# A packed-attention and expert-routing kernel: the first weight's partition layout, one slot's x turned by VectorE, and wide packing for three batches

## The chip, the cores and the metric

The kernel runs on one core of a Trainium2 chip. The metric is the device time of one execution in microseconds (us); where several runs are told, their median. Engines are named as in the profile: PE is TensorE's matmul, PEld its weight load, DVE VectorE, ACT ScalarE, POOL GpSimd, SP SyncE, which issues most of the transfers.

## The reference

Two attentions in a row, then a mixture of experts in which each token goes to one expert. B = 8 batches, 8 heads, 576 tokens, head size 64; 32 packing queries p; 8 experts, model width 512, hidden width 1024.

```python
def sm_attn(qq, kk, vv):                      # softmax(q k^T / 8) v
    ...
p_packed = sm_attn(p, k, v)                   # 32 packed rows per batch and head
out = sm_attn(q, p_packed, p_packed)
x = out.transpose(0, 2, 1, 3).reshape(B * S, H * D)        # 4608 x 512
logits = x @ w_gate + modality_bias[modality_id]
e_idx = argmax(logits); gate_w = softmax(logits)[e_idx]
for e in range(8):
    out[mask] = gate_w * (relu(x[mask] @ w1[e]) @ w2[e])   # mask: e_idx == e
```

## The kernel before, in words

**Attention.** The eight batches run as interleaved chains of small steps. The string ORDER writes out by hand in which order the steps of all batches stand on TensorE, VectorE, ScalarE and SyncE; it isn't changed. For each batch: transposes of k and q (L245), scores against p (L261), softmax, transposes of the probabilities (L285), `pack` (L307 or L301, with the scaling by VectorE at L314), `packT`, gate, scores of q against the packed rows (L261 again), a second softmax on VectorE, and `xpart` (L377), which makes x and the gate's logits. x goes to a scratch array in DRAM with one transfer per batch. `routing` (L447 and on) turns logits into list positions, and GpSimd scatters a record per token into lists by expert.

**The packing** has two forms. Narrow: four groups of matmuls with 64 input rows, 64 output rows and 128 columns, one for each pair of heads and half of the tokens. Wide: two groups with 64 input rows, 128 output rows and 256 columns, of which the two diagonal blocks are used. In the wide form VectorE's scaling takes the blocks one by one, four instructions on 64 partitions for two on 128. An fp32 matmul stands in the trace as two records. Before, `wide` held for batches 6 and 7.

**The slots.** Behind the attention, x is worked off in slots of tokens of one expert: slots 0 and 1 (256 tokens, from the first four batches, begun inside ORDER), slots 2 to 5 (256 tokens, from the first six), and then slots of up to 512 tokens. A slot fetches its rows of x by indirect DMA (L778) into `xt`, brings them into transposed order, splits them into a high and a low part (`hi` by ScalarE, `lo` by VectorE), runs `st_1` (three products with the split first weight w1) and `st_2` (three with w2), and scatters the result. Slots 0, 1 and 2 are turned by TensorE (`st_x`, L797): slots 0 and 1 through `first_x`, two tiles of 128 tokens each, and slot 2 through `st_x_both` between the two halves of slot 1's `st_2`. From slot 3 on VectorE turns them (`turn`, L813) in blocks of 32 by 32, 16 instructions for two tiles, one slot ahead, and `st_xs` (L819, L820) splits them.

**The first weight** is loaded by `load_w` with `which == 0`: 2 MB into `raw1`, from where ScalarE (L749) and VectorE (L753) split it. The order of its rows over partitions and blocks must fit that of x's columns. The scratch rows hold x as two halves u of 256 columns, so in `xt[:, t, u * HW:...]` heads lie in the order u, pair, block; the weight is fetched in that order, with eight transfers of 64 partitions.

Of the kernel before, what the change touches and what calls it, by code (L numbers as in the profile page):

```python
# [18 lines left out]
ds = bass.ds  # L19
# [5 lines left out]
def packed_attn_moe_kernel(  # L25
# [192 lines left out]
    def attention(b, lt, A, Z):  # L218
# [75 lines left out]
        def pack():  # L294
            a1T, v_t = D_["a1T"], D_["vr"]
            pp = [Z["ps1"].tile([P, 512], F32, name="ps1") for _ in range(2)]
            wide = b // 2 >= NA[1]
            for c in range(NC if wide else 0):
# [422 lines left out]
    def load_w(w, which, e):  # L721
        src, n = ((w1, KD), (w2, KF))[which]
        m = src.shape[2]
        if which == 0:
            d = w["raw1"].rearrange("p (h j f) -> p h j f", h=2, j=n)
            sv = src[ds(e, 1)].rearrange("e (a z u d) (h f) -> (e z) d h u a f", a=2, z=2, u=2, h=2)
            for h in range(2):
                for z in range(2):
                    for u in range(2):
                        ins = nc.sync.dma_start(d[64 * z:64 * z + 64, h, 2 * u:2 * u + 2], sv[z, :, h, u])  # L730
            return ins_of(ins)
        sv = src[ds(e, 1)].rearrange("a (j p) f -> p (a j) f", p=P)
        for z in range(2):
            ins = nc.sync.dma_start(w["2r"][z], sv[:, z * n // 2:(z + 1) * n // 2])
        return ins_of(ins)
# [24 lines left out]
    def fetch(tb, s, ph, mt, xt, n):  # L760
# [16 lines left out]
        def part(t, u):  # L777
            fetched.append(free(nc.gpsimd.indirect_dma_start(  # L778
                out=xt[:, t - 2 if t > 1 else 3 - t, u * HW:u * HW + HW], out_offset=None,
                in_=x_scr[0:NA[ph] * 4 * S] if ph < 2 else x_scr,  # L780
                in_offset=bass.IndirectOffsetOnAxis(ap=mt[:, t, 3 * u:3 * u + 1], axis=0))))
            return fetched[-1:]
# [12 lines left out]
    def st_x(xt, M, t, ps):  # L795
        for j in range(KD):
            nc.tensor.transpose(out=ps[:, j], in_=xt[:, t, j * P:j * P + P], identity=ident)  # L797
        yield
        ts = slice(t * P, t * P + P)
        hi, lo = (M["x"][z][:, :, ts] for z in range(2))  # L800
        ia = nc.scalar.copy(out=hi, in_=ps)
        yield
        iv = tt(out=lo, in0=ps, in1=hi.bitcast(F32), op=ALU.subtract)
        if slow[0]:
            feed(ia)
        M["ia"], M["iv"] = ins_of(ia), ins_of(iv)
        yield

    def turn(n, ts):
        g, x = (z[:, ts].rearrange("p t (j n) -> p (t j) n", n=P) for z in (xt_of(n), W["xt"][n >= SA[1]]))  # L810
        for z in range(0, P, Q):
            for w in range(0, P, Q):
                nc.vector.transpose(out=x[w:w + Q, :, z:z + Q], in_=g[z:z + Q, :, w:w + Q])  # L813

    def st_xs(M, ts):
        x = W["xt"][M is V].rearrange("p t (j n) -> p j t n", n=P)
        hi, lo = (M["x"][z].rearrange("p j (t n) -> p j t n", n=P) for z in range(2))
# [64 lines left out]

    def st_x_both(xt, M):
        for t in range(2):
            all_of(st_x(xt, M, t, W["t", t]))
        return M["ia"], M["iv"]

    def st_2(M, mt, t, op, parts=1):
# [29 lines left out]
    W["ot"] = [mxp.tile([P, DM], F32, name="ot")] * 2  # L918
    xts = [mxp.tile([P, 2, DM], F32, name=f"xt{n}") for n in range(2)]
    W["xt"] = [xts[0]]  # L920
    x_hl = mxp.tile([P, 2, KD, P2], F32R, name="x_hl")
# [5 lines left out]
    def slot_of(n):  # L927
        ph = sum(n >= z for z in first[1:])
        return T[ph]["tab"], n - first[ph], ph

    def xt_of(n):
        return xts[n % 2 if n < 3 else 1 if n < SA[1] else 2]
# [112 lines left out]
    for z, nm in enumerate(("kT", "qT")):  # L1045
# [3 lines left out]
                    "p (j n) -> p j n", j=KD)])  # L1049
    xts.append(wraw.tile([P, 4, DM], F32, name="xt2"))  # L1050
    W["xt"].append(spare("rawv", F32).rearrange("p (t f) -> p t f", t=4))
    W["ot"] = [W["ot"][0], wraw.tile([P, DM], F32, name="ot2")]

# [55 lines left out]
    def slot(n):  # L1109
# [4 lines left out]
        def x_next(done=()):  # L1114
# [3 lines left out]
            with ExitStack() as es:  # L1118
                for z in done:
                    es.enter_context(tc.issue_after(ins_of(z)))  # L1120
                after = st_xs(X, range(2 if n + 1 < SA[1] else 3))
                flag = n + 1 >= SA[1] and val(tn, sn, 6, (ET.Activation, ET.DVE), 0, 1)
            if n + 1 >= SA[1]:
                with tc.If(flag > 0):
                    turn(n + 1, slice(3, 4))
                    st_xs(V, (3,))
            return after

        if n < SA[1]:
            done = st_1_full(W)  # L1130
            if n == SA[0] - 1:
                st_2_of(n, (1, 0))
                sw(n + 1, 0, st_x_both(xts[0], X))
            else:
                sw(n + 1, 0, x_next(done))
                if n + 1 == SA[1]:
                    pending.extend(held)
                    flush()
            st_2_of(n, *(((0, 1),) if n == SA[0] - 1 else ((1, 0), (0, 1))))
        else:  # L1140
# [31 lines left out]
    def go_on(n):  # L1172
# [3 lines left out]
        if n < SA[1]:  # L1176
            if n >= SA[0]:
                turn_of(n + 1)
            pre(n + 2)
# [53 lines left out]
```

## Time and profile before

| | |
|---|---|
| time before, median of 3 runs | 565.15 us (564.54 to 567.61) |
| profiled execution | 566.15 us, span 564.5 us |
| busy share of the span: PE, DVE, ACT, POOL | 96%, 60%, 37%, 37% |
| granted TensorE clock, mean | 0.984 of 2.4 GHz |
| HBM read, written | 57.04 MB, 19.28 MB |

The span is that from the first to the last instruction; the profiled time holds 1.65 us more. Busy shares are means over stages with different limits: up to about 138 us the attention, behind it the slots.

### The profile page before, as it was taken

What the parts mean: (1) busy time and instruction counts of PE and PEld (TensorE: products, weight loads), DVE (VectorE), ACT (ScalarE), POOL (GpSimd) and SP (SyncE); (2) the same over time, 40 slices, a digit from 0 to 9 for tenths busy, and PEclk for the clock granted to TensorE, in tenths of its full rate; (3) what the DMA queues carried; (4) which work ended last, traced back from release to release, by engine and by line L of the source; (5) the groups of instructions that cost most, each with busy time, mean ns of one, the idle gap of its engine ahead of it and who ended that gap; (6) DMA issues with size and microseconds to landing.
All of it is one profiled execution on the core that took longest, in us unless ns stands there. A gap on an engine that the chain in (4) does not pass through costs nothing. (4 is left out here: it accounts for less than half of the span.)

```text
span 564.5 us, 11470 instructions
## 1 busy us (share of the span) xinstructions
PE 541.6 (96%) x4336; PEld 457.7 (81%) x4336; DVE 338.6 (60%) x760; ACT 208.9 (37%) x371; POOL 210.2 (37%) x257
## 2 busy tenths in 40 slices
PE   5999998978999999999999999999999999999995
PEld 4777777655989899899898888998888888988884
DVE  1399998997987275635576728339358148167210
ACT  2588886674532122221213224422212242422221
POOL 4002004843554445451542332473412422472402
PEclk9799999987999999999999999999999999999999
DMA  9699998993338611119621115424201210511501
GB/s 291 252 326 363 403 337 282 278 258 124 123 106 192 220 43 64 48 51 194 225 75 40 59 56 128 126 104 134 78 19 44 70 39 37 57 38 59 56 10 72
DMA packets 33684, 77.38 MB, mean 137 GB/s; under 512 B 6768, under 2 KB 6944, under 8 KB 32576
## 3 DMA queue, kind: packets, MB, share of 16 engines
q1 hardware_dynamic: 24224, 54.92, 30.5%
q0 software_dynamic: 8848, 21.28, 13.6%
q8 instruction: 43, 0.70, 0.5%
q14 instruction: 41, 0.34, 0.2%
q10 hardware_dynamic: 528, 0.13, 0.1%
HBM read 57.04 MB, written 19.28 MB: 135 GB/s over the span
## 5 line engine op out<-in xcount | busy, mean ns | idle before, releaser
L778 POOL DMA_INDIRECT xt<-x_scr,mt x86 | 85.4, 992 | 86.3 <-issue 24.5
L813 DVE STREAM_TRANSPOSE rawv<-xt 32x384 f32<-32x384 f32 (+1 forms) x192 | 92.3, 481 | 16.1 <-DMA xt<-x_scr,mt 12.3
L909 POOL DMA_INDIRECT out_dram<-ot,mt x37 | 37.3, 1008 | 138.8 <-ACT ot L898 94.3
L892 PE MATMUL ps_o<-rawq,rawk 128*128 128x512 f32 x272 | 87.2, 391 | 0.0
L856 PE MATMUL ps_h<-x_wide,w1h 128*128 128x512 f32 (+1 forms) x168 | 62.4, 371 | 0.0
L856 PE MATMUL ps_h<-x_wide,w1l 128*128 128x512 f32 (+1 forms) x168 | 61.9, 368 | 0.0
L856 PE MATMUL ps_h<-pT,w1h 128*128 128x512 f32 (+1 forms) x168 | 61.3, 365 | 0.0
L892 PEld LDWEIGHTS ps_o<-rawq,rawk 128*128 128x128 f32 x272 | 51.0, 188 | 10.4
L837 PE MATMUL ps_h<-x_hl,w1h 128*128 128x256 f32 x320 | 58.1, 283 | 0.1
L498 POOL DMA_INDIRECT lst<-meta,dsi x36 | 36.5, 1014 | 45.8 <-ACT lt L384 32.9
L837 PEld LDWEIGHTS ps_h<-x_hl,w1h 128*128 128x128 f32 x320 | 49.9, 189 | 0.6 <-DVEq L1079 0.3
L861 DVE SCALAR_TENSOR_TENSOR rawk<-ps_h,rawk 128x512 fp32r<-128x512 f32 (+1 forms) x28 | 17.4, 633 | 54.2 <-ACT rawk L860 54.0
L837 PE MATMUL ps_h<-x_hl,w1l 128*128 128x256 f32 x160 | 45.3, 284 | 0.0
L898 ACT ACTIVATE ot<-ps_o,mt 128x512 f32<-128x512 f32 x24 | 16.5, 688 | 67.8 <-PE ps_o L892 45.2
L892 PE MATMUL ps_o<-qT,rawk 128*128 128x512 f32 x96 | 37.5, 391 | 0.0
L856 PEld LDWEIGHTS ps_h<-pT,w1h 128*128 128x128 f32 x168 | 31.6, 188 | 4.1
L856 PEld LDWEIGHTS ps_h<-x_wide,w1l 128*128 128x128 f32 x168 | 31.4, 187 | 4.2
L856 PEld LDWEIGHTS ps_h<-x_wide,w1h 128*128 128x128 f32 x168 | 31.6, 188 | 3.9
L860 ACT ACTIVATE rawk<-ps_h 128x512 fp32r<-128x512 f32 (+1 forms) x28 | 15.2, 551 | 47.6 <-PE ps_h L856 46.6
L837 PEld LDWEIGHTS ps_h<-x_hl,w1l 128*128 128x128 f32 x160 | 30.2, 189 | 0.0
L892 PE MATMUL ps_t<-rawq,rawk 128*128 128x512 f32 x88 | 28.9, 389 | 0.0
L841 ACT ACTIVATE rawk<-ps_h 128x512 fp32r<-128x512 f32 x20 | 12.0, 599 | 43.4 <-PE ps_h L837 43.4
(268 smaller groups left out, 1134.2 us busy)
## 6 DMA issues: line engine op xcount, KB each, us to landing
rawq<-in_q_dram SPq DMA_DIRECT2D x8, 1152.0 KB, 9.4
rawv<-in_v_dram SPq DMA_DIRECT2D x8, 1152.0 KB, 9.6
x_scr<-xs SPq DMA_DIRECT2D x8, 1152.0 KB, 5.2
raw<-in_moe_w_dram SPq DMA_DIRECT2D x32, 256.0 KB, 7.0
rawk<-in_k_dram SPq DMA_DIRECT2D x7, 1152.0 KB, 11.7
kT<-in_moe_w_dram SPq DMA_DIRECT2D x4, 1024.0 KB, 5.5
qT<-in_moe_w_dram SPq DMA_DIRECT2D x3, 1024.0 KB, 8.1
xt<-x_scr,mt POOLq DMA_INDIRECT x86, 2.9
```

What stands on the lines that cost most here:

```text
L498: ins = ins_of(nc.gpsimd.indirect_dma_start(out=lst, out_offset=bass.IndirectOffsetOnAxis(ap=dsi[:, c:c + 1], axis=0), in_=meta[:, i * NC ...
L778: fetched.append(free(nc.gpsimd.indirect_dma_start(out=xt[:, t - 2 if t > 1 else 3 - t, u * HW:u * HW + HW], out_offset=None, in_=x_scr[0: ...
L813: nc.vector.transpose(out=x[w:w + Q, :, z:z + Q], in_=g[z:z + Q, :, w:w + Q])
L837: nc.tensor.matmul(ps[:, f], M[a][:, j, (f0 + f) * P:(f0 + f) * P + P], M["x"][b][:, j, 0:P2], start=(n == 0), stop=(n == 3 * KD - 1))
L841: ia = nc.scalar.activation(out=hid(M, "hh", f0), in_=ps, func=AF.Relu)
L856: nc.tensor.matmul(ps, M[a][:, j, f * P:f * P + P], M["x"][b][:, j, cs], start=(n == 0), stop=(n == 3 * KD - 1))
L860: ia = nc.scalar.activation(out=hh, in_=ps, func=AF.Relu)
L861: iv = nc.vector.scalar_tensor_tensor(out=hl, in0=ps, scalar=0.0, in1=hh.bitcast(F32), op0=ALU.max, op1=ALU.subtract)
L892: nc.tensor.matmul(op, hid(M, a, j, 1, slice(t * P, t * P + P))[:, 0], M[b][j // 4][:, j % 4], start=(n == 0), stop=(n == 3 * KF - 1))
L898: ia = nc.scalar.activation(out=ot, in_=op, func=AF.Copy, scale=mt.bitcast(F32)[:, row_of(t), 2:3])
L909: nc.gpsimd.indirect_dma_start(out=out, out_offset=bass.IndirectOffsetOnAxis(ap=mt[:, row_of(t), 1:2], axis=0), in_=M["ot"][t == 0], in_of ...
```

## The change

Four edits that hang together, in one diff:

- `load_w` fetches the first weight as two transfers of 128 partitions, in the natural order of its rows (row = block times 128 plus partition).
- So that x fits, `xt` is laid out as half u, tile t, column; a block of 128 columns of transposed x is made of 64 columns of each half. `st_x` makes each block with two matmuls against the identity, one for each half of the output partitions, instead of one transpose; `turn` reads the halves one by one, with as many instructions as before.
- Slot 2's x is turned by VectorE: `st_x_both` is gone, `turn` stands in slot 1's `x_next` behind slot 1's `st_1`, and both halves of slot 1's `st_2` follow each other. It turns into the first half of the buffer that the wide slots fetch into. Slot 3's `turn` is told to stand behind slot 2's last subtraction.
- `wide` holds for batches 5, 6 and 7.

```diff
-            wide = b // 2 >= NA[1]
+            wide = b >= 2 * NA[1] - 1
...
-            sv = src[ds(e, 1)].rearrange("e (a z u d) (h f) -> (e z) d h u a f", a=2, z=2, u=2, h=2)
+            sv = src[ds(e, 1)].rearrange("e (j p) (h f) -> p h (e j) f", p=P, h=2)
             for h in range(2):
-                for z in range(2):
-                    for u in range(2):
-                        ins = nc.sync.dma_start(d[64 * z:64 * z + 64, h, 2 * u:2 * u + 2], sv[z, :, h, u])
+                ins = nc.sync.dma_start(d[:, h], sv[:, h])
...
-                out=xt[:, t - 2 if t > 1 else 3 - t, u * HW:u * HW + HW], out_offset=None,
+                out=xt[:, u, t - 2 if t > 1 else 3 - t], out_offset=None,
...
         for j in range(KD):
-            nc.tensor.transpose(out=ps[:, j], in_=xt[:, t, j * P:j * P + P], identity=ident)
+            for u in range(2):
+                nc.tensor.matmul(ps[64 * u:64 * u + 64, j], xt[:, u, t, j * D:j * D + D], ident, start=True, stop=True)
...
-        g, x = (z[:, ts].rearrange("p t (j n) -> p (t j) n", n=P) for z in (xt_of(n), W["xt"][n >= SA[1]]))
-        for z in range(0, P, Q):
-            for w in range(0, P, Q):
-                nc.vector.transpose(out=x[w:w + Q, :, z:z + Q], in_=g[z:z + Q, :, w:w + Q])
+        x = turned(n)[:, ts].rearrange("p t (j n) -> p (t j) n", n=P)
+        for u in range(2):
+            g = xt_of(n)[:, u, ts].rearrange("p t (j d) -> p (t j) d", d=D)
+            for z in range(0, P, Q):
+                for w in range(0, D, Q):
+                    nc.vector.transpose(out=x[u * D + w:u * D + w + Q, :, z:z + Q], in_=g[z:z + Q, :, w:w + Q])
...
+    def turned(n):
+        return W["xt"][2 if n == SA[0] else n >= SA[1]]
...
+    W["xt"].append(xts[2].rearrange("p a b n -> p (a b n)").rearrange("p (t f) -> p t f", f=DM)[:, 0:2])
...
-                after = st_xs(X, range(2 if n + 1 < SA[1] else 3))
+                if n + 1 == SA[0]:
+                    turn(n + 1, slice(0, 2))
+                after = st_xs(X, n + 1, range(2 if n + 1 < SA[1] else 3))
...
+            W["iv"] = after[1]
             return after
...
             done = st_1_full(W)
-            if n == SA[0] - 1:
-                st_2_of(n, (1, 0))
-                sw(n + 1, 0, st_x_both(xts[0], X))
-            else:
-                sw(n + 1, 0, x_next(done))
...
-            st_2_of(n, *(((0, 1),) if n == SA[0] - 1 else ((1, 0), (0, 1))))
+            sw(n + 1, 0, x_next(done))
...
+            st_2_of(n, (1, 0), (0, 1))
...
             if n >= SA[0]:
-                turn_of(n + 1)
+                with tc.issue_after(W["iv"]) if n == SA[0] else ExitStack():
+                    turn_of(n + 1)
```

## Rows read from the trace of the kernel before

**Rows 1.** Busy time by stretch: engines' busy us, granted clock, DMA share, GB/s.

```profile
96.00:112.40 16.40, 15.33 (x235) 12.46 (x242) 15.01 (x37) 11.05 (x20) 13.96 (x32) 1.00 1.00 248
138.00:560.00 422.00, 419.82 (x2366) 365.54 (x2344) 234.20 (x520) 116.35 (x193) 166.87 (x166) 1.00 0.31 85
```

**Rows 2.** The same view of five short stretches (PE, PEld, DVE, ACT, POOL; PEclk, DMA, GB/s).

```profile
100.00:104.00 4.00, 3.83 (x71) 3.20 (x70) 3.79 (x7) 3.24 (x6) 3.63 (x9) 1.00 1.04 396
106.00:112.00 6.00, 6.00 (x102) 5.13 (x102) 5.60 (x13) 2.75 (x6) 5.04 (x7) 1.00 1.07 213
116.00:119.50 3.50, 3.50 (x36) 2.54 (x21) 3.43 (x6) 1.14 (x5) 2.89 (x3) 0.52 1.01 202
122.80:126.30 3.50, 1.72 (x25) 1.27 (x16) 3.33 (x6) 3.50 (x8) 0.00 (x0) 1.00 1.03 320
126.30:133.10 6.80, 6.57 (x30) 4.72 (x30) 4.87 (x14) 4.52 (x7) 2.08 (x3) 0.51 0.48 190
```

**Rows 3.** The first weight's transfers, 100 to 112 us: issue times, time to landing.

```profile
L730 SPq DMA_DIRECT2D raw<-in_moe_w_dram x8: 603/604/1114, 101.5 to 108.2; - x8
...
DMA to landing us min/median/max: 8.5/9.7/10.8
```

**Rows 4.** ScalarE's split of that weight: duration ns, first and last start.

```profile
L749 ACT CAST w1h<-raw x4: 1039/1052/1122, 121.5 to 129.0; 128x1024 fp32r<-128x1024 f32 x4
```

**Rows 5.** PE's instructions in order, 85 to 140 us: start, us, line, shapes.

```profile
90.69 0.48 PE L447 MATMUL ps<-lt,fold 128*64 128x72 f32 x8
91.10 1.09 PE L245 MATMUL ps<-ident,rawq 128*128 128x128 f32 x8
92.12 1.08 PE L307 MATMUL ps<-rawv,a1T 64*64 64x128 f32 x27
93.60 1.53 PE L307 MATMUL ps<-rawv,a1T 64*64 64x128 f32 x45 [0.40 <-issue]
...
106.69 4.16 PE L301 MATMUL ps<-rawv,a1T 64*128 64x256 f32 x36
...
127.20 7.78 PE L301 MATMUL ps<-rawv,a1T 64*128 64x256 f32 x36
```

**Rows 6.** DVE's instructions in order, 90 to 145 us.

```profile
95.17 0.35 DVE L314 SCALAR_TENSOR_TENSOR bd<-ps,r,mask 128x128 f32<-128x128 f32 x1 [1.14 <-PE ps L307]
...
112.47 1.44 DVE L314 SCALAR_TENSOR_TENSOR bd<-ps,r,mask 64x128 f32<-64x128 f32 x4 [0.70 <-PE ps L377]
...
128.31 0.17 DVE L451 TENSOR_TENSOR lg<-ps,bias_all 128x72 f32<-128x72 f32 x1
```

**Rows 7.** PE's instructions in order, 125 to 207 us, around the transposes of x.

```profile
139.65 1.09 PE L797 MATMUL ps<-ident,xt 128*128 128x128 f32 x8
140.68 1.62 PE L377 MATMUL ps<-bd,a2T 64*64 64x136 f32 x48
...
157.04 0.66 PE L797 MATMUL ps<-ident,xt 128*128 128x128 f32 x4
157.46 0.47 PE L892 MATMUL ps<-rawq,rawk 128*128 128x512 f32 x1
...
193.86 0.77 PE L837 MATMUL ps_h<-x_hl,w1h 128*128 128x256 f32 x5
```

**Rows 8.** DVE and ACT in order, 150 to 265 us: slots 1 and 2.

```profile
182.84 0.69 DVE L843 SCALAR_TENSOR_TENSOR rawk<-ps_h,rawk 128x512 fp32r<-128x512 f32 x1 [0.54 <-ACT rawk L841]
...
186.50 0.17 DVE L579 CAST tab_c<-tab_f 128x7 int32<-128x7 f32 x1
...
199.08 7.19 DVE L813 STREAM_TRANSPOSE xt<-xt 32x256 f32<-32x256 f32 x16 [0.45 <-DMA lst<-meta,dsi]
...
206.35 1.14 ACT L819 CAST x_hl<-xt 128x512 fp32r<-128x512 f32 x2 [0.17 <-DVE xt L813]
...
208.10 1.28 DVE L820 TENSOR_TENSOR x_hl<-xt,x_hl 128x512 fp32r<-128x512 f32 x2
```

More of the change, by code (lines that the diff above doesn't have):

```diff
@@ L809, in turn, with st_xs @@
     def turn(n, ts):
-        g, x = (z[:, ts].rearrange("p t (j n) -> p (t j) n", n=P) for z in (xt_of(n), W["xt"][n >= SA[1]]))
-        for z in range(0, P, Q):
-            for w in range(0, P, Q):
-                nc.vector.transpose(out=x[w:w + Q, :, z:z + Q], in_=g[z:z + Q, :, w:w + Q])
-    def st_xs(M, ts):
-        x = W["xt"][M is V].rearrange("p t (j n) -> p j t n", n=P)
+        x = turned(n)[:, ts].rearrange("p t (j n) -> p (t j) n", n=P)
[4 more added lines that the diff above has]
+                    nc.vector.transpose(out=x[u * D + w:u * D + w + Q, :, z:z + Q], in_=g[z:z + Q, :, w:w + Q])
+    def st_xs(M, n, ts):
+        x = turned(n).rearrange("p t (j n) -> p j t n", n=P)
         hi, lo = (M["x"][z].rearrange("p j (t n) -> p j t n", n=P) for z in range(2))
@@ L881, in st_1_full @@
         return M["last"]
[L883 to L886, printed above, removed]
     def st_2(M, mt, t, op, parts=1):
@@ L918, in packed_attn_moe_kernel @@
     W["ot"] = [mxp.tile([P, DM], F32, name="ot")] * 2
-    xts = [mxp.tile([P, 2, DM], F32, name=f"xt{n}") for n in range(2)]
-    W["xt"] = [xts[0]]
+    xts = [mxp.tile([P, 2, 2, HW], F32, name=f"xt{n}") for n in range(2)]
+    W["xt"] = [xts[0].rearrange("p a b n -> p (a b n)").rearrange("p (t f) -> p t f", f=DM)]
     x_hl = mxp.tile([P, 2, KD, P2], F32R, name="x_hl")
@@ L1049, in packed_attn_moe_kernel @@
                     "p (j n) -> p j n", j=KD)])
-    xts.append(wraw.tile([P, 4, DM], F32, name="xt2"))
+    xts.append(wraw.tile([P, 2, 4, HW], F32, name="xt2"))
     W["xt"].append(spare("rawv", F32).rearrange("p (t f) -> p t f", t=4))
+    W["xt"].append(xts[2].rearrange("p a b n -> p (a b n)").rearrange("p (t f) -> p t f", f=DM)[:, 0:2])
     W["ot"] = [W["ot"][0], wraw.tile([P, DM], F32, name="ot2")]
@@ L1125, in x_next @@
                     turn(n + 1, slice(3, 4))
-                    st_xs(V, (3,))
+                    st_xs(V, n + 1, (3,))
+            W["iv"] = after[1]
             return after
@@ L1130, in slot @@
             done = st_1_full(W)
-            if n == SA[0] - 1:
-                st_2_of(n, (1, 0))
-                sw(n + 1, 0, st_x_both(xts[0], X))
-            else:
-                sw(n + 1, 0, x_next(done))
-                if n + 1 == SA[1]:
-                    pending.extend(held)
-                    flush()
-            st_2_of(n, *(((0, 1),) if n == SA[0] - 1 else ((1, 0), (0, 1))))
+            sw(n + 1, 0, x_next(done))
+            if n + 1 == SA[1]:
+                pending.extend(held)
+                flush()
+            st_2_of(n, (1, 0), (0, 1))
         else:
```

## The prediction, made before the changed kernel ran

> **What bounds the kernel now.** The first view is the busy time of each engine by stretch. Behind 138 us TensorE works 419.8 of 422 us [rows 1]: the expert slots run as one unbroken stream of matmuls, so there the end moves only with the amount of TensorE work, or with a new wait put into the stream. Ahead of it, in the attention part, TensorE and VectorE are both nearly full (15.3 and 15.0 of 16.4 us from 96 to 112.4) [rows 1], and the order on each engine is written out by hand, so a delay there is passed on from batch to batch. The time is therefore: when the stream starts (about 138 us), what is added to it or taken from it, and the tail.
>
> The second view is the clock and the DMA traffic of short stretches [rows 2]. The reader is to see two things. The first weight moves at 213 GB/s while the DMA engines are fully busy, and other loads get 396 GB/s from equally busy engines. And TensorE's granted clock is 0.5 (1.2 GHz) in two stretches, 116 to 119.5 and 126.3 to 133.1, while it is 1.0 (2.4 GHz) in the others. Ahead of the second fall TensorE had worked 1.72 of 3.5 us. That second stretch covers the packing of the last batch, which took 7.78 us where the same 36 records of batch six took 4.16 [rows 5].
>
> The sum is made against the profiled execution: 566.15 us, a span of 564.5 and 1.65 around it. It lies 1.0 above the median of the three runs, 565.15. A difference of 0.5%, 2.8 us, is about what a measurement of this kernel can tell from no change: the bounds are 562.3 and 568.0.
>
> **The weight's load: 0.** Eight transfers of 256 KB on 64 partitions each become two of 1 MB on 128. 2.1 MB at 213 GB/s is 9.8 us, at 396 GB/s 5.3, so the weight lands some 4.5 us sooner, and SyncE issues six transfers fewer per weight at 0.6 us each [rows 2, 3]. Nobody waits for it: the last transfer is issued at 108.2 and the slowest took 10.8 us to land, so all is there by 119.0 [rows 3], and ScalarE's first split of it starts at 121.5, in its hand-written place [rows 4]. The three later loads lie under the full stream [rows 1]. If this cover were thinner than it looks, the gain would be at most those 4.5 us; I take 0. The list writes and x rows that share the DMA engines come sooner too, and this is what lets the stream start earlier, should TensorE get there earlier.
>
> **Batch five packed wide: +2.0.** The narrow packing of batch five runs from 92.12 to 95.13 with a pause of 0.40 in it; the wide one took 4.16 for batch six [rows 5]. That is +1.15, or +1.55 if the pause stays. VectorE stood waiting for it (1.14 us idle before 95.17) [rows 6], so its end is on the path. Behind it VectorE does four scalings for two; four took 1.44 us in batch six [rows 6], so two more are +0.7. Together 1.85 to 2.25. Queued behind them are the softmax steps of batches four to six and the next PSUM buffers, and with VectorE and TensorE both above 90% busy up to 112.4 there is little slack to swallow it. Bounds: 0 if all is swallowed, 2.3. I take 2.0, because the wait at 95.17 is seen.
>
> **Slot one's and two's x by matmuls: +1.5.** Eight transposes took 1.03 us (139.65 to 140.68) and four took 0.42 (157.04 to 157.46) [rows 7], so a tile costs 0.45 to 0.5. In its place come eight fp32 matmuls with 64 output rows, two records each. No such row exists with 128 columns. The nearest has the same 128x64 shape with 72 columns: eight records from 90.69 to 91.10, 51 ns each [rows 5]. Sixteen make 0.82, so +0.35 a tile and +1.4 for four; I take 1.5 for the longer rows of output. Below: the first two tiles hide behind VectorE, +0.7. Above: if the halves don't run side by side. Narrow packing has four side by side, 45 records in 1.53 us, 34 ns each [rows 5]; one at a time that is 136 ns, 2.2 us a tile, +6.8 in all.
>
> The Trainium skill speaks against this part: "TensorEngine Tiling (Array Packing)", section Tiling Modes, says that a change of tiling mode drains the TensorE. The trace doesn't show a drain: the 128x64 group of eight ends at 91.17, after the full-size transposes have started at 91.10, and so do the transposes at 140.74 against the 64x64 group at 140.68 [rows 5, 7]. As an estimate by that rule, each of eight changes would wait for the tail of the last matmul.
>
> **The third slot's x moves to VectorE: +0.5.** (Slot 2 in the code.) Eight transposes leave the stream: by the rows above 0.42 to 0.5 per four, so -0.9 [rows 7]. Slot 2's first matmul would come at 193.86 - 0.9 = 193.0 instead of 193.86 [rows 7]. Against it stand 16 block transposes on VectorE, 7.19 us as for the next slot [rows 8], then ScalarE's copies and VectorE's subtractions. They may start once slot 1's last hidden rows are done, at 183.53, or behind the table's last step, at 186.67 [rows 8]: they end at 190.7 to 193.9. One copy of 0.57 and both subtractions of 1.28 follow [rows 8], so x is ready at 192.6 to 195.8 and TensorE waits 0 to 2.8. The middle, 1.4, makes +0.5; bounds -0.9 and +1.9. What is queued behind: slot 3's block transposes, which now start at about 196 where they started at 199.08 [rows 8], so they are not late. The later slots do the same block transposes with the same sizes: 0.
>
> **The clock over the last packing: -2.6.** All of the last attention part shifts by 2 us, and whether TensorE falls to 1.2 GHz there turns on where its idle stretches fall; the rows can't settle it. At 2.4 GHz the last packing could still not run before VectorE has read the routing values that hold its second PSUM buffer, at 128.48 [rows 6]. From there it would need 3.9 (34 of 36 records of 4.16) and end at 132.4, not at 134.98 [rows 5]: -2.6. In the trace TensorE fell after a stretch half idle [rows 2]; with the wider packing it has a fuller schedule, and the earlier low stretch is not sure to come back either. So I take full clock as somewhat likelier than not.
>
> Sum: 566.15 + 2.0 + 1.5 + 0.5 - 2.6 = 567.55, so **567.5**, which is 0.4% above the median shown: no change that can be told.
>
> **The rivals.**
> *The clock falls again* (the case on the other side, slower). Place: TensorE while it packs the last batch. Price: the 2.6 are not got back, 570.2. It decides by itself: with full clock the sum is under 568.0, without it above. For it: the idle stretch before it has a cause that the change leaves alone, ScalarE being full (3.50 of 3.50 us) [rows 2]. Against: the shift.
> *The delay of batch five is swallowed*: -2.0, 565.5. For it: TensorE has a wait of its own after the narrow packing. Against: VectorE's 15.0 of 16.4 us.
> *All terms at their low ends* (faster): packing 0, first tiles +0.7, third slot -0.9, last packing -2.6, and the first low stretch gone as well, which gives back 3.5 x 0.48 = 1.7 if all of it was on the path [rows 2]. 566.15 - 4.5 = 561.6. Against: four things must go well.
> *The turn comes late on VectorE*: the full wait of 2.8, 568.9; if x comes later still, each us is one more.
> *A drained array at every change of shape*: a group's last record takes about 0.48 - 7 x 0.051 = 0.12 us [rows 5], two changes for each of four tiles, +1.0, 568.5. This is the mechanism of the rule on tiling modes named above; the overlapping starts in the trace speak against it.
> That the faster weight brings nothing is no rival here; it is in the sum.
>
> **How the numbers follow.** Forecast 0.38, the clock falls 0.22, delay swallowed 0.13, all low 0.13, late turn 0.09, drained array 0.05. Faster than 562.3: nearly all of "all low" and a little of the swallowed case, 0.14. Slower than 568.0: the clock case (0.21), most of the late turn and the drain (0.12) and the upper part of the forecast's own spread, 566 to 569 (0.11): 0.44. The rest, 0.42, is no change. The range reaches down into the all-low case and up past the clock case: 562.5 to 570.8. The upper bound of the matmul term (+6.8) lies outside it; I count it in the 2 of 10.
>
> **What would show it.** Right: the first weight's two transfers land within 6 us at about 390 GB/s; batch five's packing stands under the wide line with some 4.1 us and VectorE's scalings end about 2 us later; the first x tiles take some 0.8 us each; slot 2's first matmul waits for the subtraction, 1 to 2 us; the last packing takes 4 us behind its start and the clock there is 1.0. Wrong: if the stream starts more than 1 us before 138 in the new profile, the attention part had slack or a cost that I don't see; if TensorE's idle time behind 138 grows by over 3 us, the turn or the longer order on VectorE is the new bound; if a tile of x costs over 1.5 us, the halves don't run side by side.

## The result and the profile after

The changed kernel takes 573.04 us (median of 4 runs, 571.92 to 573.35) against 566.38 for the kernel before, run beside it (median of 4). The ratio is 1.0118, 95% interval 1.0091 to 1.0145: slower by 1.2%. The forecast was 567.5 with a range up to 570.8, so the time lies outside it on the slow side. The profiled execution took 573.19 us, its span is 571.2.

Lines move by the edit: the matmuls of x are L796, the first layer L838, the second L888, VectorE's block transposes L814. The first view is TensorE's timeline of the changed kernel (start, duration, line and operation, and in brackets the idle time before it and what ended it). It answers to [rows 5] and [rows 7].

```profile
93.25 4.16 PE L301 MATMUL ps<-rawv,a1T 64*128 64x256 f32 x36
...
99.37 0.41 PE L245 MATMUL ps<-ident,rawk 128*128 128x128 f32 x2 [0.90 <-PE ps L475]
...
127.46 1.97 PE L245 MATMUL ps<-ident,rawq 128*128 128x128 f32 x8 [2.07 <-ACT lt L384]
...
131.57 5.47 PE L301 MATMUL ps<-rawv,a1T 64*128 64x256 f32 x34 [0.30 <-DVE lg L451]
...
141.71 1.97 PE L796 MATMUL ps<-ident,xt 128*64 128x128 f32 x32
...
159.68 1.09 PE L796 MATMUL ps<-ident,xt 128*64 128x128 f32 x16
...
167.65 0.48 PE L447 MATMUL ps<-lt,fold 128*64 128x72 f32 x8
...
185.25 0.40 PE L888 MATMUL ps_o<-rawq,rawk 128*128 128x512 f32 x1
...
198.34 0.74 PE L838 MATMUL ps_h<-x_hl,w1h 128*128 128x256 f32 x4 [2.04 <-ACTq L1079]
...
199.67 0.58 PE L838 MATMUL ps_h<-x_hl,w1h 128*128 128x256 f32 x1 [0.60 <-DVEq L1079]
...
211.97 0.39 PE L888 MATMUL ps_o<-rawq,rawk 128*128 128x512 f32 x1
```

The same two marks of the second layer (slot 1's first matmul, slot 2's first) in the kernel before, and ahead of them the first transposes behind batch five's packing and the matmul that follows slot 1's x (L447):

```profile
96.08 0.44 PE L245 MATMUL ps<-ident,rawk 128*128 128x128 f32 x2 [0.27 <-DVE bd L314]
...
163.61 0.48 PE L447 MATMUL ps<-lt,fold 128*64 128x72 f32 x8
...
182.01 0.40 PE L892 MATMUL ps_o<-rawq,rawk 128*128 128x512 f32 x1
...
205.38 0.40 PE L892 MATMUL ps_o<-rawq,rawk 128*128 128x512 f32 x1
```

Four marks cut the span into stretches: the start of batch five's packing, slot 1's second layer, slot 2's second layer, the end. Before: 92.12, 182.01, 205.38, 564.5. After: 93.25, 185.25, 211.97, 571.2. The stretches grow by 1.13, 2.11, 3.35 and 0.11 us, together 6.7. Half of the loss stands between slot 1's and slot 2's second layers, the place where slot 2's x comes in. The first 1.13 lies ahead of every edited instruction.

The busy time of the engines in six stretches of the changed kernel (us; then busy time of each engine, the granted clock, DMA share and GB/s):

```profile
10.00:24.00 14.00, 10.45 (x76) 7.77 (x77) 4.23 (x9) 3.51 (x10) 1.73 (x3) 0.63 1.01 351
...
116.00:119.50 3.50, 1.76 (x44) 0.94 (x36) 3.39 (x8) 2.65 (x8) 2.59 (x4) 1.00 0.45 169
...
127.50:134.20 6.70, 6.39 (x30) 4.77 (x32) 6.35 (x16) 5.75 (x9) 3.96 (x4) 0.50 0.68 253
...
180.00:187.00 7.00, 7.00 (x54) 6.72 (x53) 5.22 (x24) 1.54 (x3) 4.62 (x5) 1.00 1.05 397
...
198.00:203.00 5.00, 4.07 (x21) 3.86 (x22) 4.76 (x14) 0.93 (x2) 4.07 (x4) 0.66 0.33 80
203.00:560.00 357.00, 357.00 (x1807) 310.69 (x1807) 188.17 (x355) 94.95 (x153) 134.96 (x135) 1.00 0.25 73
```

The low stretch from 116 to 119.5 is gone, and not only moved: from 112 to 126 the granted clock is 1.00 throughout. The clock still falls to 1.2 GHz over the last packing (0.50), as in [rows 2], and now once more behind the wait ahead of slot 2 (0.66 on average from 198 to 203). From 203 on TensorE is full.

Why does TensorE wait at 196 to 200? VectorE's timeline of the changed kernel, around the turn of slot 2's x:

```profile
186.08 0.69 DVE L844 SCALAR_TENSOR_TENSOR rawk<-ps_h,rawk 128x512 fp32r<-128x512 f32 x1 [0.54 <-ACT rawk L842]
186.68 0.15 DVE L592 TENSOR_TENSOR tab_f<-red,sidx 128x1 f32<-128x1 f32 x1
189.61 4.47 DVE L814 STREAM_TRANSPOSE xt<-xt 32x256 f32<-32x256 f32 x10 [2.78 <-issue]
...
194.37 2.70 DVE L814 STREAM_TRANSPOSE xt<-xt 32x256 f32<-32x256 f32 x6
...
198.95 0.67 DVE L821 TENSOR_TENSOR x_hl<-xt,x_hl 128x512 fp32r<-128x512 f32 x1
```

The turn could begin at 186.8 and begins at 189.61. Its 7.4 us and the subtractions end at 199.6, where TensorE had run dry at 196.3. GpSimd's and SyncE's timelines, and the landing times (issues from 173.9 to 175; last number is the median from issue to landing in us), tell what the turn waited for:

```profile
174.05 0.75 POOL L769 DMA_DIRECT2D mt<-lst  x1 [1.80 <-DMA lst<-meta,dsi]
...
181.14 1.00 POOL L776 DMA_INDIRECT xt<-x_scr,mt  x1 [4.59 <-issue]
```

```profile
173.54 1.13 SPq L728 DMA_DIRECT2D raw<-in_moe_w_dram  x2
176.00 1.08 SPq L732 DMA_DIRECT2D kT<-in_moe_w_dram  x1
177.43 0.37 SPq L732 DMA_DIRECT2D qT<-in_moe_w_dram  x1
```

```profile
mt<-lst POOLq DMA_DIRECT2D x1, 4.0 KB, 6.3
```

The row list (4 KB) is issued 0.5 us behind the first weight's 2 MB, and the second weight's 2 MB follow from 176.00 on: the list lands after 6.3 us. Only then can the four gathers of x go, at 181.14, with the weights still moving at 397 GB/s. GpSimd's and SyncE's timelines of the kernel before have the other order:

```profile
170.02 0.75 POOL L771 DMA_DIRECT2D mt<-lst  x1 [1.81 <-DVE inc L467]
...
172.91 0.99 POOL L778 DMA_INDIRECT xt<-x_scr,mt  x1 [0.39 <-issue]
```

```profile
170.77 7.41 SPq L730 DMA_DIRECT2D raw<-in_moe_w_dram  x8
187.34 0.42 SPq L734 DMA_DIRECT2D kT<-in_moe_w_dram  x1
```

There the list goes 0.75 us ahead of the weight, lands in 2.1 us, and the second weight comes 11 us later than in the changed kernel. Counted from the first weight's first transfer, it is issued 16.6 us later there and 2.5 us later in the changed kernel. Of the 14.1 us between them, 6.3 are issue time (7.41 and 1.13 us); 7.5 are a wait of SyncE behind the eight transfers, which it doesn't have behind the two. What it waits for there the profile doesn't tell.

### The profile page after: what moved, and what is told of

Read it like the earlier page. It is cut to its first block, busy times and chain, and to the rows that moved or that the text cites. A ratio compares the mean times of both kernels' runs of the same rounds, so it can differ in the third digit from the quotient of the medians.

```text
span 571.2 us, 11327 instructions
## 1 busy us (share of the span) xinstructions
PE 544.0 (95%) x4340; PEld 460.1 (81%) x4340; DVE 347.2 (61%) x778; ACT 208.9 (37%) x371; POOL 208.6 (37%) x257
## 5 line engine op out<-in xcount | busy, mean ns | idle before, releaser
L814 DVE STREAM_TRANSPOSE rawv<-xt 32x384 f32<-32x384 f32 (+1 forms) x192 | 92.3, 481 | 10.7 <-DMA xt<-x_scr,mt 6.5
L888 PE MATMUL ps_o<-rawq,rawk 128*128 128x512 f32 x272 | 86.4, 390 | 0.0
L838 PE MATMUL ps_h<-x_hl,w1h 128*128 128x256 f32 x320 | 59.3, 287 | 2.6 <-ACTq L1079 2.0
L888 PEld LDWEIGHTS ps_o<-rawq,rawk 128*128 128x128 f32 x272 | 51.1, 188 | 10.5
L838 PEld LDWEIGHTS ps_h<-x_hl,w1h 128*128 128x128 f32 x320 | 50.8, 193 | 3.5 <-ACTq L1079 2.5
L838 PE MATMUL ps_h<-x_hl,w1l 128*128 128x256 f32 x160 | 45.8, 287 | 0.0
L888 PE MATMUL ps_o<-qT,rawk 128*128 128x512 f32 x96 | 37.5, 390 | 0.0
L814 DVE STREAM_TRANSPOSE xt<-xt 32x256 f32<-32x256 f32 x64 | 27.9, 436 | 6.3 <-issue 2.8
L838 PEld LDWEIGHTS ps_h<-x_hl,w1l 128*128 128x128 f32 x160 | 30.8, 193 | 0.0
L844 DVE SCALAR_TENSOR_TENSOR rawk<-ps_h,rawk 128x512 fp32r<-128x512 f32 x20 | 13.7, 690 | 26.2 <-ACT rawk L842 25.9
```

The lines of the kernel that those rows point to most:

```text
L814: nc.vector.transpose(out=x[u * D + w:u * D + w + Q, :, z:z + Q], in_=g[z:z + Q, :, w:w + Q])
L838: nc.tensor.matmul(ps[:, f], M[a][:, j, (f0 + f) * P:(f0 + f) * P + P], M["x"][b][:, j, 0:P2], start=(n == 0), stop=(n == 3 * KD - 1))
L844: iv = nc.vector.scalar_tensor_tensor(out=hid(M, "hl", f0), in0=ps, scalar=0.0, in1=hid(M, "hh", f0).bitcast(F32), op0=ALU.max, op1=ALU.su ...
L888: nc.tensor.matmul(op, hid(M, a, j, 1, slice(t * P, t * P + P))[:, 0], M[b][j // 4][:, j % 4], start=(n == 0), stop=(n == 3 * KF - 1))
```

## The experiments

The theory: slot 2's x rows are late, because weights stand ahead of the row list and the gathers. The rivals: VectorE's turn is too long whatever the rows do; the attention part (wide packing, matmuls of x) is the main loss. All ratios are to the kernel before on the same chip. The table has the marks as above, read from each kernel's TensorE timeline: A is from batch five's packing to slot 1's second layer, B from there to slot 2's.

| kernel | median us | ratio, 95% interval | A | B |
|---|---|---|---|---|
| before | 566.4 to 567.0 | 1 | 89.89 | 23.37 |
| changed | 573.04 | 1.0118, 1.0091 to 1.0145 | 92.00 | 26.72 |
| held_both | 569.00 | 1.0038, 1.0022 to 1.0054 | 92.33 | 22.35 |
| held_w2 | 568.27 | 1.0031, 1.0017 to 1.0046 | 92.10 | 22.53 |
| x_tr | 567.75 | 1.0018, 0.9999 to 1.0037 | 92.37 | 22.33 |
| x2_pe | 575.32 | 1.0145, 1.0118 to 1.0172 | 95.14 | 29.54 |
| x2_pe_order | 570.82 | 1.0069, 1.0048 to 1.0091 | 94.97 | 25.48 |
| narrow5 | 572.26 | 1.0096, 1.0068 to 1.0123 | 91.03 | 27.62 |
| narrow5_held | 567.72 | 1.0028, 1.0009 to 1.0046 | 88.92 | 23.27 |
| wide5_only | 569.58 | 1.0067, 1.0040 to 1.0093 | 93.69 | 23.37 |
| load_only | 565.83 | 0.9981, 0.9959 to 1.0003 | 87.83 | 23.37 |
| load_128 | 597.51 | 1.0554, 1.0528 to 1.0579 | 120.98 | 23.37 |
| slot2_dve | 597.70 | 1.0538, 1.0512 to 1.0564 | 121.32 | 22.33 |
| slot2_dve_held | 597.21 | 1.0546, 1.0524 to 1.0567 | 120.83 | 22.35 |

**The weights held back.** Both kernels are the changed one; held_both holds both weights, held_w2 the second alone.

```diff
+        behind_x = lambda i: (tc.add_manual_dep(ins_of(i), fetched[11].name, SYNC, reason="x first")
+                              if 12 <= len(fetched) < 17 and (True, True)[which] else None)
...
                 ins = nc.sync.dma_start(d[:, h], sv[:, h])
+                behind_x(ins)
...
```

(fetched[11] is the last gather of slot 2's x; held_w2 has (False, True).)

> The changed kernel, with the three transfers behind the second expert list's first weight and its second weight (two of 1 MB for the first, two of 1 MB for the second, issued at 173.5 to 177.4 in the changed kernel) made to wait for the last gather of slot 2's x rows. Late x rows (the theory): the row list lands some 3 us behind its issue in place of 6.3, the gathers start at about 177.5 in place of 181.1, VectorE's block transposes start right behind the last hidden rows (within 0.5 us, where they waited 2.8), TensorE's stall ahead of slot 2 is under 1 us in place of 3.05, the clock doesn't fall there, and the time is 569 to 570.5 (573.0 less 2.6 to 4.1). Turn too long on VectorE (rival): the block transposes start sooner, but TensorE still waits 2.5 us or more, and the time is 572 or more. Attention part (rival): the same, since the 6.7 us lie ahead of 138 us.

> The changed kernel, with the second weight's two transfers alone (issued at 176.0 and 177.4) made to wait for the last gather of slot 2's x rows; the first weight's two, issued just ahead of the row list, stay in front. Late x rows: 2 MB in place of 4 stand in the DMA queues when the row list is issued; it already lay behind the first weight alone, so it lands only a little sooner, but the gathers then meet an empty queue; the block transposes start 1.5 to 2.8 us sooner, time 569.5 to 571.5. If the second weight is what matters: the same as with both held. If VectorE's turn itself is too long: 572 or more.

Both lose the wait, and 4.0 and 4.8 us of the time. held_both lands at the lower edge of its range; held_w2 is 1.2 us faster than its own and takes the case named for it, that the second weight is what matters. Stretch B falls from 26.72 to 22.35 and 22.53, below the 23.37 of the kernel before. VectorE's turn alone doesn't make TensorE wait, so the second rival falls; the third falls for this half of the loss. held_w2 also shows how the two delays add. Its GpSimd, VectorE and landing rows (issues from 172 to 174, then from 180 to 186):

```profile
173.12 0.75 POOL L772 DMA_DIRECT2D mt<-lst  x1 [1.80 <-DMA lst<-meta,dsi]
...
180.61 1.00 POOL L779 DMA_INDIRECT xt<-x_scr,mt  x1 [5.01 <-issue]
```

```profile
185.15 0.69 DVE L847 SCALAR_TENSOR_TENSOR rawk<-ps_h,rawk 128x512 fp32r<-128x512 f32 x1 [0.30 <-ACT rawk L845]
...
185.98 4.47 DVE L817 STREAM_TRANSPOSE xt<-xt 32x256 f32<-32x256 f32 x10
```

```profile
mt<-lst POOLq DMA_DIRECT2D x1, 4.0 KB, 6.7
...
xt<-x_scr,mt POOLq DMA_INDIRECT x4, 2.7
```

The list is as late as in the changed kernel (6.7 us), for the first weight is still ahead of it. But the gathers, with no second weight beside them, land in 2.7 us where they took 5.7, and the turn starts at once. Late list plus slow gathers is too much; with batch five packed wide, either alone is not.

**Why the list lost its place.** x_tr turns x of slots 0 and 1 by transposes again; x's columns come out in another order than the weight's rows there.

```diff
-            for u in range(2):
-                nc.tensor.matmul(ps[64 * u:64 * u + 64, j], xt[:, u, t, j * D:j * D + D], ident, start=True, stop=True)
+            nc.tensor.transpose(out=ps[:, j], in_=xt[:, j // 2, t, j % 2 * P:j % 2 * P + P], identity=ident)
```

> The changed kernel, with slot 0's and 1's x turned by whole 128x128 transposes of the same buffer, eight a pair of tiles as before; the columns of x come out in another order than the weight's rows in these two slots. Direct gain, from the rows: 1.0 us a pair in the first two tiles (1.97 against 1.09) and 0.6 for each later one, at most 2.1, net 1.2 as measured at slot 1's second half. If the row list was overtaken because slot 1's x delays GpSimd's chain (tile out, list, row list) by 1.2 us and SyncE's weight load not: the row list is issued ahead of the weight again, the stall of 3.05 us ahead of slot 2 and the clock's 1.3 us go as well, and the time is 567 to 568.5. If the order of the two issues has another cause: 571 to 572.

567.75, inside the first of the two ranges, and B is 22.33. GpSimd's and SyncE's timelines, and the landing of that list:

```profile
172.58 0.75 POOL L769 DMA_DIRECT2D mt<-lst  x1 [1.80 <-DVE inc L467]
```

```profile
173.33 1.13 SPq L728 DMA_DIRECT2D raw<-in_moe_w_dram  x2
```

```profile
mt<-lst POOLq DMA_DIRECT2D x1, 4.0 KB, 2.1
```

The list goes 0.75 us ahead of the weight, as in the kernel before, and lands in 2.1 us. Slot 1's matmuls of x take 1.09 us a tile where the transposes take 0.66 [rows 7]; they delay slot 0's tiles, their way out and the list behind them on GpSimd. Against x_tr, the list is issued 1.47 us later in the changed kernel (174.05 for 172.58), the load 0.21 (173.54 for 173.33). Some 1.3 us in the wrong chain turned the order of the two issues round, and that cost more than the matmuls themselves. The gathers take 6.9 us here beside the same 4 MB; starting at 175.44, they are in time.

**Slot 2's x on TensorE.** The changed kernel with slot 2's x turned by the new matmuls.

```diff
-            sw(n + 1, 0, x_next(done))
+            if n == SA[0] - 1:
+                st_2_of(n, (1, 0))
+                sw(n + 1, 0, st_x_both(xts[0], X))
...
-                with tc.issue_after(W["iv"]) if n == SA[0] else ExitStack():
-                    turn_of(n + 1)
+                turn_of(n + 1)
```

(The second hunk, by which slot 3's turn is no longer held behind slot 2's subtraction, is in x2_pe alone.)

> The changed kernel, with slot 2's x turned on TensorE as before (by the new matmuls with 64 output rows), between the tiles of slot 1's second half. Late x rows, with the turn's 8 us on VectorE as the amplifier: the x rows land at the same late time, 187 to 190, but TensorE wants them only about there; +2.0 for two tiles of matmuls, -3.05 of stall, -1.3 of clock, and so 570 to 571.5. If the late rows alone decide: TensorE waits 2 us or more ahead of these matmuls, and the time is 573 or more.

> As x2_pe, but with slot 3's block transposes kept behind slot 2's last subtraction on VectorE, as in the changed kernel. In x2_pe two of them stood ahead of the subtraction and waited 7.3 us for slot 3's rows, and TensorE waited 2.4 us for the subtraction. Late rows with the turn as amplifier: without that order TensorE doesn't wait ahead of slot 2, and the time is 570 to 571.5 (573.0 + 2.0 - 3.05 - 1.3, and 0.9 either way for the start and the clock of the last packing). Late rows alone decide: TensorE waits ahead of the x matmuls or behind them 2 us or more, 573 or more.

x2_pe missed: 575.32. VectorE's and TensorE's timelines show why, and it was an artifact of how I undid the part:

```profile
199.23 0.88 DVE L814 STREAM_TRANSPOSE xt<-xt 32x256 f32<-32x256 f32 x2 [7.30 <-PE ps_o L893]
200.12 0.69 DVE L802 TENSOR_TENSOR x_hl<-ps_t,x_hl 128x512 fp32r<-128x512 f32 x1
```

```profile
204.28 0.39 PE L838 MATMUL ps_h<-x_hl,w1h 128*128 128x256 f32 x1 [2.42 <-DVEq L1084]
```

Two transposes of slot 3, whose gathers were only issued from 193.78 on, stood ahead of the subtraction for slot 2. With the order kept (x2_pe_order) the wait is gone and the time is 570.82, inside what was expected. The rows are late here too: the list is issued at 176.30, 0.5 us behind the weight, and the gathers start at 183.42. B is 25.48, 3.15 above the 22.33 of the kernels with no x in this part of TensorE's stream; the records of the two tiles, in three pieces, fill 2.4 of that. So TensorE's later use of x hides the late rows: its first x matmul comes 4.2 us behind the start of slot 1's second layer (191.68 against 187.49). VectorE's turn wants them 1.5 us behind it (186.8 against 185.25), and that made them a wait. A isn't to be compared here: in both profiles it is 3 us longer than in the changed kernel, through the clock (0.61 on average from 126 to 139, 0.81 to 0.85 from 142 to 146, against 0.74 and 1.00), and the profiled execution of x2_pe_order took 573.71, 2.9 above its median.

**The wide packing of batch five**, undone in the changed kernel (narrow5), undone with the second weight held (narrow5_held), and done alone in the kernel before (wide5_only).

```diff
-            wide = b >= 2 * NA[1] - 1
+            wide = b // 2 >= NA[1]
```

> The changed kernel, with batch five packed narrow as before. Batch five costs 2.2 of the 6.7 us (from the compared traces); everything behind it shifts together, so the row list stays behind the weight and the stall ahead of slot 2 stays at 2.5 to 3.5: 570 to 571.3. With the last packing at 2.4 GHz up to 2 less. Delay swallowed (rival): 572.5 or more.

> The changed kernel, with batch five packed narrow and the second weight's two transfers held behind slot 2's gathers. By the sum of the parts: 568.3 (held alone) less 2.0 to 2.2 is 566.1 to 566.3, no difference from the kernel before: what is left is +1.2 for the matmuls of x in slots 0 and 1, -0.9 for slot 2's transposes and 0 to -0.8 for the faster first weight. If the parts don't add up (the packing's delay swallowed once the stall is gone): 567.8 or more.

> The kernel before with the wide packing from batch five on, and nothing else. Batch five costs what the comparison shows: its packing takes 4.2 us, the transposes behind it start 2.0 to 2.3 us later, and of that 1 to 2 us is left at the start of the expert slots, so 567.4 to 568.6. Delay swallowed (rival): 566.4 within 0.6. If the clock falls differently in the last batch, that is up to 2.6 either way, to be read from the granted clock of the last packing.

narrow5 gives back only 0.8 us, less than expected: A is 0.97 shorter, but B 0.90 longer. VectorE's turn begins at 189.79, against 189.61 in the changed kernel: with the rows late, what is gained ahead of them is waited away. wide5_only loses 0.67%, more than expected. Its last packing runs at full clock, and what that brings goes into a wait for slot 0's x, in TensorE's timeline:

```profile
130.46 4.15 PE L301 MATMUL ps<-rawv,a1T 64*128 64x256 f32 x34 [0.22 <-DVE lg L451]
...
142.28 0.44 PE L797 MATMUL ps<-ident,xt 128*128 128x128 f32 x2 [2.04 <-DMA xt<-x_scr,mt]
```

The clock is low again behind that wait (48 records of L377 take 2.66 us, 1.62 in the kernel before [rows 7]).

narrow5_held is 1.5 us above the sum of the parts, and 0.28% slower than the kernel before. Half of the 1.5 stands in B, 23.27 against held_w2's 22.53: VectorE is free sooner with the narrow packing, the list is issued 0.5 us behind the weight as in the changed kernel, and the turn waits 0.83 us for its rows (it begins at 184.48). So in the medians undoing batch five gives back 0.8 us, or 0.5 with the second weight held (567.72 against 568.27), where the traces price it at 2 us and more; what the rest of the difference is stays open.

The packing's own price is best read where the last packing ran at the low clock in both: x_tr (wide, 7.88 us) against before (narrow, 7.78 [rows 5]), A 92.37 against 89.89, +2.5; the load differs between these two as well. The matmuls of x: narrow5 (7.75) against before, 91.03 against 89.89, or at full clock, with one load in both, narrow5_held against load_only, 88.92 against 87.83. Both give +1.1. The first pair is the cleaner one, for load_only has a wait of 0.68 us for slot 0's x among its transposes. As far as the two tell, the load has no part in A.

**The load alone**, in the kernel before, whose x keeps its order.

```diff
-            sv = src[ds(e, 1)].rearrange("e (a z u d) (h f) -> (e z) d h u a f", a=2, z=2, u=2, h=2)
+            sv = src[ds(e, 1)].rearrange("e (j p) (h f) -> p h (e j) f", p=P, h=2)
             for h in range(2):
-                for z in range(2):
-                    for u in range(2):
-                        ins = nc.sync.dma_start(d[64 * z:64 * z + 64, h, 2 * u:2 * u + 2], sv[z, :, h, u])
+                ins = nc.sync.dma_start(d[:, h], sv[:, h])
```

> The kernel before with the two-transfer load of the first weight alone; x keeps its old order of columns, so the weight's rows don't match it. As the prediction has it (nobody waits for the weight): 0, that is 566.4 within 1.0, and slot 2's x is on TensorE when it is wanted. Late x rows: SyncE is done with the first weight 6 us sooner here too and sends the second weight right behind it, so the row list and the gathers for slot 2 land 3 to 6 us later than before; the transposes of slot 2's x, at 182.8, wait for them 0 to 3 us, time 566.5 to 569.5.

565.83, no difference that can be told (0.9959 to 1.0003). The second weight is sent behind the first at once here too (172.26), but the list went ahead (169.03, landed in 2.1 us), and B is 23.37 as before. In this execution the last packing ran at full clock (4.15 us for 34 records behind a wait of 1.31); whether the load had a part in that is open.

**The load over 128 partitions in the old order**, with and without slot 2's turn on VectorE.

```diff
...
-                        ins = nc.sync.dma_start(d[64 * z:64 * z + 64, h, 2 * u:2 * u + 2], sv[z, :, h, u])
+                        ins = nc.sync.dma_start(d[:, h, 2 * u + a], sv4[:, :, h, u, a])    # two runs of 64 rows
```

> The kernel before, its eight transfers of 256 KB of the first weight kept, each of one block of rows over 128 partitions in place of two blocks over 64; the order of rows and x stays, and so the output. If the 213 GB/s came from the 64 partitions: 350 to 400 GB/s while they run, and the weight is there 3 to 4 us sooner; if from the number or size of the transfers: 213 again. Nobody waits for the weight: 565.8 to 566.9, as for the load alone in two transfers (565.8) or no change.

> As load_128, and slot 2's x turned on VectorE as in the changed kernel; slots 0 and 1 keep their transposes and batch five its narrow packing. Here GpSimd's chain isn't delayed, so the row list goes ahead of the weight, x's rows are at hand, and the move alone costs what the prediction gave it: -0.9 of transposes and 0 to 0.5 of a wait, 565.3 to 566.5. If the turn on VectorE is itself too long: a wait of 2 us or more ahead of slot 2, 568 or more.

> As slot2_dve, with the second weight's two transfers held behind slot 2's gathers. If the rows are at hand anyway: the same as slot2_dve within 0.6, 565.3 to 566.5, and against the kernel before 0 to -1.4. If slot2_dve shows a wait for rows, this takes it away.

All three take 597, 30 us more, and none of the expectations held. SyncE's timeline, the busy time from 104 to 136, and who waited for the weight, in load_128:

```profile
101.30 35.48 SPq L730 DMA_DIRECT2D raw<-in_moe_w_dram  x8
```

```profile
104.00:136.00 32.00, 16.48 (x284) 11.97 (x269) 17.11 (x33) 10.04 (x22) 18.85 (x22) 0.78 0.23 75
```

```profile
who waited for it (us, times):
  ACT w1h L749: 31.7, 1
```

The DMA engines are busy for 23% of that time, and ScalarE's first split waits 31.7 us for a weight that nobody waited for before. The three kernels still compare among themselves: with slot 2's x on VectorE, and the rows there in time, B is 22.33 against 23.37. The move by itself gives 1.0 us. In the medians (597.70 against 597.51) it doesn't show.

**Three more, on another chip.** slot2_old is the kernel before with slot 2's turn alone moved; slow_load is the changed kernel with eight transfers over 64 partitions.

```diff
-            sv = src[ds(e, 1)].rearrange("e (j p) (h f) -> p h (e j) f", p=P, h=2)
+            sv = src[ds(e, 1)].rearrange("e (u a z d) (h f) -> (e z) d h u a f", a=2, z=2, u=2, h=2)   # slow_load
...
```

> The kernel before, with its own load of the first weight, its transposes for slots 0 and 1 and its narrow packing; only slot 2's x is turned on VectorE. The row list goes ahead of the weight, so by the prediction's term the move is worth -0.9 of transposes and costs 0 to 2.8 of a wait: 565.8 to 566.5 if x's rows are at hand when the last hidden rows are done, up to 568.7 if the turn alone is too long.

> As slot2_old, with the second weight's two transfers held behind slot 2's gathers. In the kernel before they were issued behind the gathers anyway (187.3), so no difference from slot2_old within 0.6. If it is faster by 1 us or more, the rows were late in slot2_old too.

> The changed kernel, its weight rows and x in their new order, but the first weight loaded by eight transfers of 256 KB over 64 partitions as before. If 4 MB in front of the row list is what counts (faster issue and the second weight right behind): SyncE needs 7 us for the eight issues, the second weight comes behind the gathers, the row list waits for some 256 KB only, the gathers start 2 to 4 us sooner than in the changed kernel, TensorE's stall ahead of slot 2 is 0 to 1.5, and the time is 568.5 to 571. If the matmuls of slots 0 and 1 suffice by themselves to put the rows late: 572.5 to 574.

This chip ran the kernel before at 580.4 us, so the microseconds expected don't apply, and only ratios count: slot2_old 1.0029 (1.0004 to 1.0053), slot2_old_held 1.0013 (0.9987 to 1.0040), slow_load 1.0112 (1.0068 to 1.0156). Moving slot 2's x brings nothing here, with or without the second weight held; B is 23.33 and 22.88, and there is no trace of the kernel before on this chip to set beside them. slow_load is as slow as the changed kernel, against what I expected of it, though its turn didn't wait for rows. VectorE's, TensorE's and ScalarE's timelines:

```profile
202.76 0.68 DVE L846 SCALAR_TENSOR_TENSOR rawk<-ps_h,rawk 128x512 fp32r<-128x512 f32 x1
203.43 4.46 DVE L816 STREAM_TRANSPOSE xt<-xt 32x256 f32<-32x256 f32 x10
```

```profile
212.17 0.74 PE L840 MATMUL ps_h<-x_hl,w1h 128*128 128x256 f32 x4 [1.24 <-ACTq L1081]
```

```profile
199.90 1.09 ACT L844 ACTIVATE rawk<-ps_h 128x512 fp32r<-128x512 f32 x2 [4.93 <-remote]
```

TensorE's wait there is 1.24 and 0.36 in place of 2.04 and 0.60, but it has another cause. ScalarE stood still for 4.93 us ahead of slot 1's last hidden rows, released by something that the profile doesn't name; so they were done 3.6 us behind the start of slot 1's second layer (199.88), against 1.5 us in the changed kernel, and the turn followed at once. This execution took 591.34, 4.8 above the kernel's median. So slow_load shows rows in time, but what the slower load is worth stays open, here and on the first chips. No kernel here beats the kernel before by more than its interval.

## Why the prediction was wrong

The span grew by 6.7 where the terms gave 1.4 (2.0 + 1.5 + 0.5 - 2.6). Point by point:

- **The weight's load, 0:** right for the load by itself (load_only). The rate was right too (382 to 401 GB/s from 108 to 112), though the two transfers took 9.5 and 12.5 us to land, not 6. The term asks only who waits for the weight, and leaves the later loads as lying "under the full stream"; that x rows sharing the DMA engines "come sooner too" is wrong for slot 2. With two transfers SyncE sent the second weight 11 us earlier (176.0 against 187.3), right on top of the gathers.
- **Batch five, +2.0:** right in the traces, +2.5 by x_tr against before; the medians gave back less (narrow5, narrow5_held). VectorE's wait and scalings moved what stands behind the packing by 2.16 us (96.08 to 99.37, less 1.13 of the start).
- **x of slots 0 and 1 by matmuls, +1.5:** +1.1 in A, near by luck. The halves run side by side, sixteen records in about 1 us, but a tile of slot 1 costs 0.70 us more than by transposes, twice the term's 0.35: from the first of the two tiles to L447 it is 7.97 us (159.68 to 167.65) against 6.57 (157.04 to 163.61). The first two tiles add 0.60 (138.71 to 145.26, from the last batch's packT to slot 0's first matmul, against 136.66 to 142.61). Of these 2.0, 0.8 was got back between L447 and slot 1's second layer, where the kernel before has waits (0.28 us ahead of 170.05). The term missed the matmuls' second effect, the delay of GpSimd's chain past SyncE's load.
- **The third slot's x, +0.5:** the step that failed. It measured +3.35. The gain was right (-1.04, predicted -0.9). The wait was sized from when VectorE is free, "once slot 1's last hidden rows are done", with x's rows taken as at hand. They were 2.8 us late, because the row list stood behind the first weight and the gathers ran beside the second, and the sum of the wait and the low clock behind it is 4.39 (26.72 less 22.33), where the term had 1.4 and its bound 2.8. The rival "The turn comes late on VectorE" had the mechanism in half a sentence ("if x comes later still, each us is one more") and 0.09 of the chance. Held weights take it away: 568.3 to 569.0, close to the forecast, though not by its terms, for the clock's -2.6 wasn't reached and slot 2's part was below the +0.5.
- **The clock, -2.6:** not reached. The last packing took 1.22 and 5.47 us, mostly still at 1.2 GHz, while the first low stretch [rows 2] was gone. What is left of A's +2.11 after +2.5 and +1.1 is -1.5, a remainder and no run's measure. The rows show most of it: the last packing, counted from A's start, begins 0.5 us sooner than x_tr's, in which the first low stretch is not gone (granted clock 0.88 from 112 to 126, as before), and from its start to its end it takes 6.99 us for the 7.78 of before.
- **The start, +1.1, not in the sum:** ahead of all edits. TensorE's granted clock from 10 to 24 us is 0.63 in this execution and 0.76 in that of before; it is 0.63 in load_only and 0.76 in held_w2 as well, with and without the change. It goes with the execution, not with the edit.
- **The drained array:** not settled. What four tiles cost TensorE, +2.0, is more than the 1.4 worked out without a drain. The sixteen records take 64 ns each (163.69 to 164.71) and not 51, and the step to them from the last 128x512 record is 0.32 us (163.37 to 163.69), where the step to the transposes is 0.23 (160.08 to 160.31 in the kernel before). That is about 0.1 us at such a change of shape, near the rival's 0.12; whether it is a drain no run shows.

Together: 1.1 + 2.5 + 1.1 - 1.5 + 3.35 + 0.1 = 6.65, the span's 6.7.

## What to carry to other kernels

Where a transfer is made faster or cheaper to issue, write down what its queue sends next and who else uses the DMA engines then; here a 4 KB list that four gathers hang on was hurt most. Where work moves to an engine that needs its input earlier, the input's arrival is a term of its own, read from the landing times and not from when the engine is free. And when chains on two engines race for one resource, a delay of a microsecond in one of them is worth what the lost order costs, not a microsecond.

## What the hardware did that I had not expected

A 4 KB row list took 2.1 us to land with nothing ahead of it (before, x_tr, load_only) and 6.3 to 6.7 us when 2 MB of weights had been issued 0.5 to 0.8 us earlier on another engine's queue. The Trainium skill, "DMA: Bandwidth & Descriptors", section Queues, rings and completion order, says that each DMA engine takes its queues in turn, packet by packet; the list's 4 us more show that a short transfer on its own queue isn't spared by that.

Eight transfers of 256 KB to 128 partitions, each from two runs of 64 rows, took 35 us to issue, with the DMA share at 0.23 from 104 to 136 and 0.15 from 120 to 130, where the eight transfers to 64 partitions were issued from 101.5 to 108.2 [rows 3]. The same page, section Why a DMA increments its semaphore by 16 and not by 1, says that a transfer runs on the largest number of engines, up to 16, that divides the slowest dimension of both its source and its destination; the source's is 2 here, which would put it on two engines of sixteen, a share of 0.125 as an estimate. The 0.15 agrees, with some other traffic beside it; the rows don't show single engines.
